# A long convolution factored 64 x 64 instead of 256 x 16, with its first and last stage as eight array pieces

## The chip, the cores and the metric

The kernel runs on one core of a Trainium2 chip. The metric is device time in microseconds (us) of one execution, the median of three runs. The names of the engines are those of the profile: PE is TensorE's matrix array and PEld its weight load, DVE is VectorE, ACT is ScalarE, POOL is GpSimd, SP is the engine that only issues transfers. DMA stands for the sixteen transfer engines that carry what SP and POOL issue.

## The reference

Two independent sequence models run on inputs of 2048 positions x 1024 channels in bfloat16. Their outputs stand side by side.

```
# A: a gated long convolution
k_shift = sum over t<4 of k_pad[:, t:t+S, :] * shift_k[:, 3 - t]
kv = k_shift * v
y  = irfft(rfft(kv, 2S) * rfft(ssm_k, 2S))[:S] + kv * ssm_D     # causal, per channel
a  = q * y
# B: a diagonal complex recurrence
Bu = einsum(x, B_bar);  h = Lam_bar * h + Bu[t] for every t
b  = 2 * Re(einsum(hs, C)) + x * Dskip
out = concatenate([a, b], -1)
```

## The kernel before, in words

**Part A** is a transform of 4096 points in two factors, done by matrix products. Before the change the factors are 256 and 16 (`N1, N2 = 256, 16`). Position s is 16 n + n2: partition n (128 of them), step n2 (16 of them).

- *kv.* `kp` and `vp` load two steps of k and v on 128 partitions each, in one transfer on SP's queue (a k block shifted by one position in two). `kvm`, `kva`, `kvb`, `kvc` form one kv tile [128, 1024] for each n2 on DVE.
- *First stage of kv.* `am` multiplies a kv tile by the 128 x 128 tables F1 (cosine, sine): four matmuls of 512 columns for each n2, 64 in all (L580). `ae` evicts each bank on ACT, `ast` stores to DRAM (Ys_kv) on POOL's queue.
- *First stage of the filter.* `hl` loads ssm_k, `hT` transposes it on PE, `hc` evicts, `hm` multiplies by F1 (128 matmuls of 256 columns, L619), `he` evicts, `hst` stores to Ys_h in two transfers (L632).
- *Second stage.* For each of 16 groups gq of two rows: `lh`, `lk` load (L642), `sh`, `sk` multiply by tables of 64 columns (two column pieces of the array side by side, L650), `she`, `ske` evict, `pr` multiplies spectra on DVE, `sa` multiplies back (two row pieces of 64 partitions, L680), `sae` evicts, `vst` stores to Vs.
- *Output stage.* `vl` loads, `a3` multiplies by the table G (two accumulating matmuls of 512 columns for each half tile, 64 in all, L706), `a3e` evicts, `qp` loads q, `qm` multiplies by q on DVE (L716), `ost` stores (L718).

All of Ys must be stored before the second stage can load, and all of Vs before the output stage: two barriers through DRAM.

**Part B** goes in 16 chunks i of 128 positions. `x` loads a transposed chunk, `U` projects it (2048 matmuls of 128 columns, L469), `ue` evicts, `r1`, `r2` rotate on DVE, `rc` adds the carry, `sc` scans, `cm`, `ca` make the next carry, `r3`, `r4` rotate back, `y` projects out (L524, L529), `ye` evicts, `yst` stores. B has no barrier, and its work lies between that of A.

**Order.** Nothing is planned while the kernel runs. The string `ORDER` is a list of some 1700 words such as `am.0.0:p6`, each a call of the function of that name, and the program is emitted in that order. Each engine and each queue then runs its own instructions strictly in that order and waits where an input or a buffer is missing. What follows the colon are the buffers: `p` is one of eight PSUM banks, `a`, `b`, `m`, `w` are rings in SBUF.

SP carries all loads, POOL all stores. At the end each engine drains (L780).

Of the kernel before, what the change touches and what calls it, by code (L numbers as in the profile page):

```python
# [67 lines left out]

ORDER = """
ld_w:a0a1 wb.3:p0 wb.2:p1 wb.0:p2 wb.1:p3 wbe.1 bl.3.1:b0 wb.7:p4 bl.3.0:b1 ld_par par_T:p5 p32 exp1 dve2 exp2 wbe.3 dve3 wbe.2 wb.4:p6 wbe.4  # L70
bl.2.1:b2 bT.2.1:p3 sm_pre bT.3.0:p5 bc.3.0 tabA1:a0a2a3a4 sin0 wbe.7 bl.4.0:b3 bT.4.0:p0 bc.4.0 bl.0.1:b4 bl.2.0:b5 bl.1.0:b6 bT.2.0:p6 wb.5:p5
bc.2.0 bT.3.1:p1 bT.0.1:p4 bl.0.0:b7 bT.0.0:p7 bc.0.0 bc.2.1 sin1 bT.1.0:p0 x.3:b8 U.3.1.0:p3 wb.6:p6 bc.3.1 U.3.1.1 bl.1.1:b9 bT.1.1:p7 bc.0.1 wbe.5
bc.1.0 wbe.6 x.1:b10 U.1.0.0:a1p5 tabA2 wbe.0 U.1.1.0:p0 U.1.1.1 x.2:b2 U.2.1.0:p2 bc.1.1 U.3.0.0:a5p7 ue.3.1 U.2.0.0:a6p3 U.2.0.1 sin2 par_rest eo
kp.1 U.2.1.1 ue.2.1 ue.2.0 z1 kp.0 dd kvm.3:m0 bl.5.0:b0 cl.2.0:b4 bT.5.0:p6 kva.3 kvb.3:b9 bc.5.0 x.0:b5 U.0.0.0:a7p4 U.0.0.1 bl.7.1:b6 U.0.1.0:p3
U.0.1.1 bl.4.1:b7 bT.4.1:p2 U.1.0.1 stt bc.4.1 ue.0.0 kp.-1 bl.5.1:b3 U.3.0.1 ue.3.0 bl.6.0:b1 ue.1.0 kvm.1:m0 cl.2.1:b11 bT.6.0:p2 bT.5.1:p4 bc.5.1
bc.6.0 U.0.2.0:p6 kva.1 kvb.1:b3 z2 cT.2.1:p5 bT.7.1:p7 bc.7.1 bl.6.1:b12 bT.6.1:p4 bc.6.1 kp.-2 kvm.0:m1 kva.0 kvb.0:b12 U.0.2.1 bl.7.0:b13 vp.0:a8
cT.2.0:p2 kvc.1 U.3.2.0:p1 cl.1.0:b14 bT.7.0:p7 U.3.2.1 bc.7.0 vp.1:a9 ue.1.1 ue.0.1 U.1.3.0:p4 U.1.3.1 U.0.3.0:p3 ue.0.2 ue.1.3 kvc.0 ld_F am.0.0:p6
cl.1.1:b0 ae.0.0:b13 U.0.3.1 ue.0.3 kvm.2:m1 cT.1.0:p4 cc.1.0 r1.0:m0 am.0.2:p6 cl.3.1:b7 cT.3.1:p0 x.4:b1 cc.3.1 ae.0.2:b7 cT.1.1:p3 cc.1.1
U.4.0.0:a8p7 cc.2.1 cl.3.0:b11 U.3.3.0:p4 U.3.3.1 ue.3.3 cT.3.0:p6 kva.2 kvb.2:b0 U.4.0.1 kvc.2 ue.4.0 cl.0.0:b6 cT.0.0:p5 cc.0.0 r2.0:a7 cl.0.1:b4
cc.2.0 sc.0.0 am.1.2:p4 am.0.1:p3 U.1.2.0:p0 ae.1.2:b6 U.1.2.1 ae.0.1 cT.0.1:p5 cc.3.0 am.1.3:p2 ast.0.0 sc.0.1 cm.0 ae.1.3 ast.1.1 r3.0:m0 r4.0  # L80
am.0.3:p7 ae.0.3 ast.0.1 U.2.2.0:p4 U.2.2.1 cc.0.1 ue.1.2 am.2.0:p2 r1.1:m1 r2.1:a0 ae.2.0:b12 U.4.3.0:p6 cx.7.0 hl.1.0:a4 U.4.3.1 ue.4.3 hl.0.0:a2
hl.0.1:a3 hT.0.0:p0 hc.0.0:b4 hl.1.1:a10 hT.1.3:p2 hT.1.0:p5 hc.1.0:b13 ld_sd hd.0 am.1.0:p6 ue.3.2 ae.1.0:b6 am.1.1:p7 ae.1.1 am.2.1:p3 ast.1.0
ae.2.1 hd.1 U.2.3.0:p0 hc.1.3:b7 hT.0.2:p5 hc.0.2:b3 U.4.2.0:p1 U.4.2.1 ue.4.2 U.2.3.1 hm.0.0.2:p2 he.0.0.2:b11 x.5:b14 U.5.0.0:a1p3 hm.0.0.3:p1
he.0.0.3 kvc.3 ca.0 rc.1 lw.2:w0 sc.1.0 hm.0.0.0:p5 he.0.0.0:b6 sc.1.1 y.0.0.0:p2 y.0.0.1 U.5.0.1 ast.2.0 hst.0.0.1 cm.1 hm.0.0.1:p5 ue.2.2 ue.2.3
r1.2:m1 hm.0.2.0:p4 cx.5.1 lw.1:w1 hm.1.0.0:p0 he.1.0.0:b4 he.0.0.1 r3.1:m0 am.2.2:p1 ae.2.2:b12 cx.4.1 am.2.3:p7 ae.2.3 y.0.0.2 y.0.0.3 hm.0.2.2:p1
hm.1.0.1:p5 cx.6.0 U.5.3.0:p7 hm.1.3.2:p0 r2.2:a6 ca.1 ast.2.1 he.1.0.1 hst.1.0.0 rc.2 hst.0.0.0 hm.1.0.3:p5 he.0.2.0:b11 hm.0.2.3:p6 hm.0.2.1:p4
he.0.2.2:b0 he.0.2.3 hst.0.2.1 U.5.3.1 r4.1 he.0.2.1 r1.3:m1 ue.5.3 sc.2.0 sc.2.1 cm.2 hT.0.3:p6 ca.2 hm.1.0.2:p4 U.5.2.0:p1 ue.5.0 he.1.3.2:b3
hT.1.2:p3 he.1.0.2:b13 r2.3:a5 rc.3 hm.1.3.0:p0 he.1.3.0:b12 he.1.0.3 hm.1.3.1:p7 he.1.3.1 y.1.0.0:p4 kp.3 hT.1.1:p0 hc.1.1:b4 hst.1.0.1 cx.6.1
hc.0.3:b6 U.5.1.0:p5 U.5.1.1 hm.1.1.3:p0 ue.5.1 cx.4.0 cx.5.0 cx.7.1 y.1.1.0:p7 hm.1.1.2:p5 ye.0.0:b0 hm.1.3.3:p6 he.1.3.3 hst.1.3.1 y.1.0.1
he.1.1.2:b7 he.1.1.3 lw.0:w2 hst.1.1.1 kp.2 kvm.4:m0 hT.0.1:p2 hc.0.1:b13 hc.1.2:b3 y.0.1.0:p6 hm.0.3.2:p0 y.0.1.1 hst.0.2.0 hm.1.1.0:p2 he.1.1.0:b5  # L90
y.0.1.2 hst.1.3.0 y.0.1.3 ye.0.1 hm.0.3.3:p5 he.0.3.2:b7 y.1.0.2 U.5.2.1 y.1.0.3 sc.3.0 ue.5.2 hl.2.1:a9 hm.0.3.0:p2 hm.0.3.1:p6 he.0.3.0:b6 kva.4
hm.1.1.1:p3 he.1.1.1 y.1.1.1 hl.2.0:a4 hT.2.3:p2 hT.2.0:p3 yst.0 he.0.3.3 he.0.3.1 hst.0.3.0 hc.2.0:b12 hm.1.2.3:p5 hm.1.2.2:p1 hst.1.1.0 he.1.2.2:b10
he.1.2.3 r3.2:m1 ye.1.0:b4 y.1.1.2 y.1.1.3 ye.1.1 U.4.1.0:p1 yst.1 U.4.1.1 hc.2.3:b0 hst.1.2.1 hm.0.1.0:p7 sc.3.1 cm.3 hst.0.3.1 ca.3 vp.4:a10 hd.2
hm.2.0.3:p4 hm.2.0.2:p2 hm.2.3.0:p5 he.2.3.0:b11 he.2.0.2:b6 he.2.0.3 hst.2.0.1 hl.3.0:a2 r4.2 y.2.0.0:p3 y.2.0.1 r3.3:m1 r4.3 hm.2.0.0:p2 he.2.0.0:b5
hm.2.3.2:p4 vp.2:a3 kvm.5:m1 hm.1.2.0:p5 hm.2.3.1:p6 he.2.3.1 hm.2.0.1:p0 he.2.0.1 kvb.4:b10 y.2.0.2 he.1.2.0:b12 ue.4.1 y.2.0.3 am.3.0:p0 ae.3.0:b4
kvm.6:m0 kva.6 hst.2.3.0 hm.0.1.1:p5 hm.1.2.1:p6 he.1.2.1 am.3.1:p1 he.0.1.0:b7 he.0.1.1 he.2.3.2:b3 hst.2.0.0 hst.0.1.0 hl.3.1:a7 hT.3.0:p2
y.2.1.0:p0 y.2.1.1 y.2.1.2 hc.3.0:b6 hst.1.2.0 am.3.2:p2 kvc.4 ae.3.1 ast.3.0 ye.2.0:b2 hd.3 hm.0.1.2:p4 hm.2.3.3:p1 hm.0.1.3:p5 he.0.1.2:b11 he.0.1.3
am.3.3:p7 y.2.1.3 am.4.3:p4 am.4.2:p5 ae.4.2:b5 ae.4.3 y.3.0.0:p3 y.3.0.1 ast.4.1 ae.3.2:b9 ae.3.3 ast.3.1 hm.3.0.2:p4 kvb.6:b0 hm.3.0.0:p2 ye.2.1
he.2.3.3 hst.2.3.1 kva.5 am.4.0:p5 ae.4.0:b12 kvb.5:b13 am.4.1:p7 kvc.5 yst.2 vp.3:a0 kvc.6 am.6.2:p6 hst.0.1.1 he.3.0.2:b10 ae.4.1 hm.3.0.3:p0
# [685 lines left out]
```

## Time and profile before

| | |
|---|---|
| median of three runs | 390.47 us (389.85 to 391.01) |
| the profiled execution | 391.46 us, of it 389.7 us of span |
| PE busy | 363.3 us, 93% of the span |
| DVE busy | 332.3 us, 85% |
| ACT busy | 278.1 us, 71% |
| POOL busy | 93.0 us, 24% |
| TensorE clock granted, mean | 0.992 |
| DMA | 92.49 MB, 237 GB/s on average |

The span is from the first to the last instruction. Durations of matmuls in the profile are modelled and overlap; how long one holds the array is seen from the distance between starts. In a row of a group the numbers behind the first bar are the group's busy time in us and the mean ns of one, behind the second bar the idle time of its engine just before them and what ended it. In a timeline row stand start, length, engine, line, operation and count.

### The profile page before, as it was taken

Reading aid. Unit: us, or ns where it says so; the run is one execution under the profiler, and the core shown is the slowest. Engines: PE = TensorE matmul, PEld = TensorE weight load, DVE = VectorE, ACT = ScalarE, POOL = GpSimd, SP = SyncE. Lnnn points to the kernel's source line nnn. Section 1 sums busy time; section 2 is a strip of 40 time slices with the busy share of each in tenths; the row PEclk is TensorE's granted clock in tenths of the full one; section 3 lists DMA queues with packets and bytes.
Section 4 is the critical chain, followed back from the end, with each engine's and each line's share of the span. In section 5 each row is a group of like instructions: output and inputs, shape, how many; then the busy total and the mean of one; then the engine's idle time right before and its main releaser. Section 6 shows DMA issues by size and latency. Waiting matters only on the chain.

```text
span 389.7 us, 9237 instructions
## 1 busy us (share of the span) xinstructions
PE 363.3 (93%) x3785; PEld 244.9 (63%) x3785; DVE 332.3 (85%) x335; ACT 278.1 (71%) x519; POOL 93.0 (24%) x156
## 2 busy tenths in 40 slices
...
GB/s 231 276 301 316 296 181 250 200 228 234 278 205 318 211 238 226 163 274 219 280 204 212 126 208 283 255 145 280 200 275 150 334 109 277 286 252 307 267 319 80
DMA packets 56005, 92.49 MB, mean 237 GB/s; under 512 B 30078, under 2 KB 32126, under 8 KB 55964
## 3 DMA queue, kind: packets, MB, share of 16 engines
...
q14 instruction: 12, 0.10, 0.1%
...
## 4 chain that ended last, share of the span: by engine, by line
PE 51%; ACT 14%; issue 12%; DVE 10%; DMA 9%; POOL 2%; POOLq 0%; ACTq 0%; DVEq 0%
PE ps_y L524 18%; PE ps_u L469 15%; PE ps_a L680 4%; PE ps_a L650 4%; DMA Ys_h<-ysbh 4%; ACT hh L657 3%; PE ps_a L619 3%; PE ps_a L580 3%; ACT xx L663 3%; DVE mt L560 2%; DMA Ys_kv<-ysb 2%; ACT vsb L687 2%; DMA out_dram<-ot 2%; DVE mt L567 2%; POOL out_dram L718 1%
## 5 line engine op out<-in xcount | busy, mean ns | idle before, releaser
L524 PE MATMUL ps_y<-CT,h 128*128 128x512 bf16 x512 | 127.0, 379 | 0.3 <-ACT ot L712 0.2
L469 PE MATMUL ps_u<-xT,BT 128*128 128x128 bf16 x2048 | 124.7, 219 | 0.6 <-ACT BT L445 0.3
L469 PEld LDWEIGHTS <-BT 128*128 128x128 bf16 x2048 | 118.4, 98 | 10.5 <-issue 4.1
L524 PEld LDWEIGHTS <-h 128*128 128x128 bf16 x512 | 45.2, 98 | 45.0 <-issue 2.4
L500 DVE TENSOR_TENSOR_SCAN h<-rtab,h 128x1024 bf16<-128x1024 f32 x32 | 71.9, 2279 | 0.3
L471 ACT CAST u<-ps_u 128x512 bf16<-128x512 f32 x64 | 38.6, 628 | 33.0 <-PE ps_u L469 24.4
L632 POOL DMA_DIRECT2D Ys_h<-ysbh x64 | 46.1, 722 | 29.0 <-ACT ysbh L625 23.3
L625 ACT CAST ysbh<-ps_a 128x512 bf16<-128x512 f32 x64 | 35.6, 616 | 16.9 <-PE ps_a L619 6.6
L481 DVE TENSOR_TENSOR mt<-u,Z 128x4096 bf16<-128x4096 bf16 x16 | 36.5, 2281 | 9.6 <-ACT u L471 9.6
L587 ACT CAST ysb<-ps_a 128x512 bf16<-128x512 f32 x64 | 35.5, 630 | 8.2 <-PE ps_a L580 4.1
L689 POOL DMA_DIRECT2D Vs<-vsb x16 | 8.5, 534 | 122.8 <-ACT vsb L687 96.7
L657 ACT CAST hh<-ps_a 128x512 bf16<-128x512 f32 x64 | 36.0, 649 | 2.3 <-PE ps_a L650 2.2
L589 POOL DMA_DIRECT2D Ys_kv<-ysb x32 | 17.5, 551 | 81.4 <-ACT ysb L587 81.4
L481 DVE TENSOR_TENSOR mt<-h,Z 128x4096 bf16<-128x4096 bf16 x16 | 36.6, 2287 | 0.2
L687 ACT CAST vsb<-ps_a 128x512 bf16<-128x512 f32 x64 | 34.2, 694 | 3.3 <-PE ps_a L680 3.3
L663 ACT CAST xx<-ps_a 128x512 bf16<-128x512 f32 x64 | 35.8, 660 | 0.6 <-PE ps_a L650 0.6
L535 ACT CAST yo<-ps_y 128x512 bf16<-128x512 f32 x32 | 19.5, 626 | 16.4 <-PE ps_y L524 16.3
L560 DVE TENSOR_TENSOR mt<-kring,wbc 128x4096 bf16<-128x4096 bf16 (+3 forms) x16 | 30.1, 1884 | 0.1
L529 PE MATMUL ps_y<-Dd,xT 128*128 128x128 bf16 x128 | 28.0, 219 | 0.0
L619 PE MATMUL ps_a<-hT,F1t 128*128 128x256 bf16 x128 | 20.5, 272 | 5.6 <-ACT hT L607 3.6
L712 ACT CAST ot<-ps_a 128x512 bf16<-128x512 f32 x32 | 17.4, 606 | 10.7 <-PE ps_a L706 6.3
L670 DVE TENSOR_TENSOR pp<-xx,hh 128x2048 bf16<-128x2048 bf16 x16 | 19.4, 1220 | 6.0 <-ACT xx L663 3.5
...
## 6 DMA issues: line engine op xcount, KB each, us to landing
...
l2h<-Ys_h SPq DMA_DIRECT2D x16, 512.0 KB, 5.7
l2k<-Ys_kv SPq DMA_DIRECT2D x16, 512.0 KB, 4.6
Vs<-vsb POOLq DMA_DIRECT2D x16, 512.0 KB, 5.4
...
kring<-in_A_k_dram SPq DMA_DIRECT2D x8, 512.0 KB, 4.3
v<-in_A_v_dram SPq DMA_DIRECT2D x8, 512.0 KB, 5.9
```

The lines of the kernel that those rows point to most:

```text
L469: nc.tensor.matmul(pu[:, w, jl, :], BT[:, 2 * jp + jl, w, d, :], xT[:, d, :], start=(d == 0), stop=(d == ND - 1))
L471: E["ue"] = lambda i, jp: nc.scalar.copy(st["u", i][:, :, 2 * jp:2 * jp + 2, :], st["pu", i, jp][:])
L481: nc.vector.tensor_mul(m, s_, win(Z))
L500: nc.vector.tensor_tensor_scan(gf, rt1, gf, 0.0, ALU.mult, ALU.add)
L524: nc.tensor.matmul(py[:], h[:, 1 - w, j, :], CT[:, j, w, dh * 512:(dh + 1) * 512], start=(j == 0 and w == 0), stop=(j == NJ - 1 and w == 1))
L560: nc.vector.tensor_mul(m[:, 0:h0, :], kring[:, s0:s0 + h0, :], wbc[:, 0:h0, :])
L587: nc.scalar.copy(st["ysb", n2, cc][:, dh * 512:(dh + 1) * 512], st["pa", n2, w][:])
L625: nc.scalar.copy(st["yh", qd, n4, w // 2][:, :, w % 2, :], st["pa", qd, n4, w][:].rearrange("p (c d) -> p c d", c=2))
L632: gpd(Ys_h[cc, n0:n0 + 2, :, qd * DQ:(qd + 1) * DQ].rearrange("n k d -> k n d"), t_[:, cc, :, :])
L657: nc.scalar.copy(st["hh", gq][:, cc, w * 512:(w + 1) * 512], st["ps", "l2h", gq, cc, w][:])
L663: nc.scalar.copy(st["xx", gq, cc][:, w * 512:(w + 1) * 512], st["ps", "l2k", gq, cc, w][:])
L687: nc.scalar.copy(st["vsb", gq][:, gi, w * 512:(w + 1) * 512], st["ps", "v", gq, w][gi][:])
```

## The change

The factors become 64 and 64. Position s is 64 n + 16 q + s': the partition is 4 n + q for the filter, and 32 q + n for k, v, q and the output, so that the four quarters q of 32 partitions hold four independent small transforms of 32 rows (n) and 64 results (32 frequencies, real and imaginary). What it does in each place:

- `am` takes two kv tiles and 512 columns: eight matmuls of 32 rows x 64 columns of the array, four row groups (one for each quarter q, each with a bank of its own) and two column groups (one for each tile). 16 calls for 64 matmuls before.
- `a3` likewise: eight matmuls of 64 rows x 32 columns, two banks, 16 calls for 64 matmuls.
- `hm` keeps 128 x 128, with a block table Fht, and takes 512 columns: 64 matmuls for 128. `hst` stores in one transfer where it took two.
- `kp`, `vp`, `qp`, `ost`: four transfers of 32 partitions each for one of 128. `lh`, `lk`, `vst`: two transfers of one group row each for one of both. `vl`: 16 transfers of 512 KB for 32 of 256 KB.
- `qm` multiplies [128, 2048], 8 times for 16.
- ost.2, ost.3 and yst.11, 13, 14, 15 are stored from SP's queue.
- The whole list `ORDER` is new. In it kv tiles 10 and 11 come last in the first stage (before: tile 14), and the store of `ost.5` is the last word.

```diff
-N1, N2, NFFT = 256, 16, 4096
-NG = 32
+N1, N2, NFFT = 64, 64, 4096
+HK = N1 // 2
+NB = 16
...
+SP_STORES = frozenset("ost.2 ost.3 yst.11 yst.13 yst.14 yst.15".split())
...
+kva.11 kvb.11:b2 kvc.11 U.11.2.0:p3 ...
+... am.5.0:p5p2p6p7 ae.5.0.0:b8 am.5.1:p4p0p3p1 ae.5.1.0 ast.5.0 U.8.1.0:p5
+U.8.1.1 ... U.11.1.0:p4 U.11.1.1 ae.5.0.3:b3 ae.5.1.3 lh.2:a7 sh.2.0.0:p3 ...
...
+... r3.15:m1 r4.15 y.15.1.0:p7 a3e.3.1.0 y.15.0.0:p5
+y.15.0.1 y.15.0.2 y.15.0.3 y.14.0.2 a3e.2.1.0 qp.6:a11 y.14.0.3 qm.6 ost.6 y.15.1.1 yst.12 y.15.1.2 qp.0:a13 qm.0 ost.0 qp.1:a3 qm.1 yst.11 ost.1
+qp.3:a7 qm.3 ost.3 a3e.2.0.1 qm.2 ost.2 y.14.1.2 y.15.1.3 ye.15.0:b6 ye.14.0:b4 ye.15.1 yst.15 y.14.1.3 ye.14.1 yst.14 ost.5
...
+    stq = lambda kind, n: spd if "%s.%d" % (kind, n) in SP_STORES else gpd
...
+    Ys_kv = tc.dram_tile([NB, HK, 2, 4, D], BF16, name="Ys_kv")
+    Ys_h = tc.dram_tile([NB, HK, 2, 4, D], BF16, name="Ys_h")
+    Vs = tc.dram_tile([NB, HK, 2, 4, D], BF16, name="Vs")
+    kr, vr, qr, oar = (a_.rearrange("(n q s) d -> q n s d", q=4, s=NB) for a_ in (k, v, q, out_a))
...
+    def quarters(t_, src, r):
+        for q_ in range(4):
+            spd(t_[32 * q_:32 * q_ + 32, :, :], src[q_, :, 2 * r:2 * r + 2, :])
...
-        st["pa", n2, w] = ptile("ps_a", [P, 512])
-        nc.tensor.matmul(st["pa", n2, w][:], F1t[:, cc, :], st["kv", n2][:, dh * 512:(dh + 1) * 512], start=True, stop=True)
+    def pieces(banks, rows, weights, cols):
+        m = weights.shape[-1]
+        for r, pt in enumerate(banks):
+            rs = slice(rows * r, rows * r + rows)
+            for j in range(P // m):
+                nc.tensor.matmul(pt[m * j:m * j + m, :], weights[rs, :], cols(j, r)[rs], start=True, stop=True)
+
+    def am(u, w):
+        st["pa", u, w] = [ptile("ps_a", [P, 512]) for _ in range(4)]
+        pieces(st["pa", u, w], 32, F1t[:], lambda j, r: st["kv", 2 * u + j][:, w * 512:(w + 1) * 512])
...
+    def ast(u, r):
+        gpd(Ys_kv[2 * u:2 * u + 2, :, :, r, :].rearrange("t k c d -> (t k c) d"), st["ysb", u, r][:])
...
+        nc.tensor.matmul(pt[:], Fht[:, kh, :], st["hT", qd, n4][:, 2 * tp:2 * tp + 2, :].rearrange("p a b -> p (a b)"), start=True, stop=True)
...
+        dst = Ys_h[4 * n4:4 * n4 + 4, 16 * kh:16 * kh + 16, :, :, qd * DQ:(qd + 1) * DQ]
+        gpd(dst.rearrange("t k c q d -> (k c q) t d"), st["yh", qd, n4, kh][:])
...
-        spd(st[nm, gq][:], Ys.rearrange("c n (s g) d -> (c n s) g d", g=NG)[:, gq * GC:(gq + 1) * GC, :])
+        for gi in range(GC):
+            spd(st[nm, gq][:, gi, :], Ys[:, gq * GC + gi, :, :, :].rearrange("t c q d -> t (c q) d"))
...
+    def vl(u, h):
+        st["vv", u, h] = k4("vv", [P, 2, D])
+        spd(st["vv", u, h][:], Vs[2 * u:2 * u + 2, :, :, 2 * h:2 * h + 2, :].rearrange("t k c q d -> (t k c) q d"))
...
+    def a3_(u, w):
+        st["po", u, w] = [ptile("ps_a", [P, 512]) for _ in range(2)]
+        pieces(st["po", u, w], 64, Gt[:], lambda j, r: st["vv", u, j // 2][:, j % 2, w * 512:(w + 1) * 512])
...
+    def ost(u):
+        for q_ in range(4):
+            stq("ost", u)(oar[q_, :, 2 * u:2 * u + 2, :], st["ot", u][32 * q_:32 * q_ + 32, :, :])
```

More of the change, by code (lines that the diff above doesn't have):

```diff
@@ L84 @@
[L84 to L87, printed above, removed]
@@ L92 @@
[L92 to L95, printed above, removed]
@@ L96 @@
[L96 to L99, printed above, removed]
@@ new lines @@
+he.1.2.0:b3 ye.1.1 hm.1.2.1:p2 he.1.2.1 y.0.1.0:p6 x.5:b0 hst.1.2.0 hm.1.1.0:p0 he.1.1.0:b9 he.1.1.1 hl.2.0:a8 r4.2 hm.1.2.3:p3 y.0.1.1 vp.4:a4
+hm.1.1.2:p2 y.0.1.2 he.1.2.2:b12 he.1.1.2:b11 hm.1.1.3:p0 hl.3.1:a10 U.5.3.0:p4 he.1.1.3 hst.1.1.1 hm.0.1.1:p0 kvb.3:b13 r3.3:m0 yst.1 U.5.1.0:p2
+y.0.1.3 he.1.2.3 ye.0.0:b14 ye.0.1 hm.0.1.0:p5 hm.0.1.2:p7 he.0.1.0:b10 he.0.1.1 hst.0.1.0 U.4.2.0:p3 hl.2.1:a5 hT.2.0:p5 hc.2.0:b3 hst.1.1.0 cm.3
+hd.2 U.4.2.1 ue.4.2 r1.4:m1 r4.3 hm.0.1.3:p0 he.0.1.2:b6 he.0.1.3 hst.0.1.1 yst.0 U.5.0.0:a0p1 lw.1:w1 vp.1:a7 kvc.3 U.5.0.1 ue.5.0 hst.1.2.1 U.5.1.1
```

347 lines of the change are left out of this document (157 added, 190 removed).

## The prediction

> **What bounds the kernel now.** The page's first part comes first, then the engines' busy time by stage, the stages cut where the first and the last matmul of the conv's second stage run (first L650, last L680) and where the last matmul ends.
>
> ```profile
> span 389.7 us, 9237 instructions
> ## 1 busy us (share of the span) xinstructions
> PE 363.3 (93%) x3785; PEld 244.9 (63%) x3785; DVE 332.3 (85%) x335; ACT 278.1 (71%) x519; POOL 93.0 (24%) x156
> ```
> ```profile
> core 0: us, PE busy (x) PEld busy (x) DVE busy (x) ACT busy (x) POOL busy (x), PEclk, DMA share, GB/s
> 0.00:183.30 183.30, 168.02 (x2099) 135.31 (x2099) 164.13 (x198) 141.88 (x250) 69.02 (x112) 1.00 0.87 244
> 183.30:317.70 134.40, 133.43 (x1234) 74.93 (x1234) 124.87 (x98) 108.51 (x217) 10.60 (x20) 1.00 0.66 218
> 317.70:380.40 62.70, 61.88 (x458) 34.68 (x456) 43.33 (x41) 27.16 (x53) 12.86 (x24) 1.00 0.82 284
> 380.40:389.70 9.30, 0.00 (x0) 0.00 (x0) 0.00 (x0) 0.57 (x1) 0.54 (x1) 0.66 0.18 67
> ```
>
> From 183.3 us to 380.4 us TensorE (PE) is busy 195.3 of 197.1 us: there its work is the time. Before 183.3 us two engines share the bound, PE with 168.0 and VectorE (DVE) with 164.1 of 183.3 us. After the last matmul 9.3 us follow in which only one eviction and one store run. So the change has to be priced three times: in PE work, in what DVE lets through in stage one, and in the end.
>
> What a matmul occupies is read from the spacing of starts, not from the modelled duration. The timeline of PE shows full-array matmuls and the two kinds of half-array pieces that the kernel has already:
>
> ```profile
> 190.00 0.22 PE L529 MATMUL ps_y<-Dd,xT 128*128 128x128 bf16 x1
> 190.06 2.97 PE L524 MATMUL ps_y<-CT,h 128*128 128x512 bf16 x13
> 192.87 0.83 PE L469 MATMUL ps_u<-xT,BT 128*128 128x128 bf16 x12
> ```
> ```profile
> 248.14 0.61 PE L680 MATMUL ps_a<-pp,wts 64*128 64x512 bf16 x4
> 248.57 0.61 PE L680 MATMUL ps_a<-hh,wts 64*128 64x512 bf16 x4
> 249.11 0.41 PE L650 MATMUL ps_a<-l2h,wts 128*64 128x512 bf16 x2
> 249.35 0.60 PE L650 MATMUL ps_a<-l2k,wts 128*64 128x512 bf16 x4
> 249.78 0.38 PE L650 MATMUL ps_a<-l2h,wts 128*64 128x512 bf16 x2
> 250.10 0.29 PE L469 MATMUL ps_u<-xT,BT 128*128 128x128 bf16 x2
> ```
>
> Thirteen full 512-column matmuls take 192.87 - 190.06 = 2.81 us, 0.216 us each; a 128-column one takes 0.06 us. Four row pieces (64*128) take 248.57 - 248.14 = 0.43 us and four column pieces (128*64) 249.78 - 249.35 = 0.43 us: two pieces run in the time of one matmul, in either direction. A change of the array's cut costs: the last row pair starts 0.22 us after 248.57 and the next kind should follow at 249.01, but starts at 249.11; the last column pair starts at 249.78 and L469 follows after 0.32 instead of 0.216 us. I take 0.10 us per change of cut.
>
> **The change part by part, on PE.**
>
> ```profile
> L619 PE MATMUL ps_a<-hT,F1t 128*128 128x256 bf16 x128 | 20.5, 272 | 5.6 <-ACT hT L607 3.6 <-ACT ysb L587 1.5
> L580 PE MATMUL ps_a<-acc,F1t 128*128 128x512 bf16 x64 | 20.1, 379 | 3.6 <-DVE mt L567 2.7 <-ACT ysbh L625 0.7 <-DVE acc L575 0.2
> L706 PE MATMUL ps_a<-vv,Gt 128*128 128x512 bf16 x64 | 16.3, 379 | 0.6 <-ACT ot L712 0.6
> ```
>
> kv's first stage (am): 64 x 0.216 = 13.8 us go; 16 calls of eight 32*64 pieces come. If all eight run side by side a call takes 0.216 us and a little for issuing eight; I take 0.24 (an estimate), 3.8 us. The new order puts the 16 calls in 13 separate places, each with a change of cut before and after: 26 x 0.10 = 2.6 us. Net -7.4 us, all in stage one.
>
> Output stage (a3): 64 x 0.216 = 13.8 us go; 16 x 0.24 = 3.8 us come, in 7 places, 14 x 0.10 = 1.4 us. Net -8.6 us, all after the second stage.
>
> The second stage's calls stay, but the new order breaks them into 30 runs of one cut where the old one has 25; with neighbours counted that is 54 changes against 44, +1.0 us. The filter's first stage (hm) has the same columns, 128 x 256 before and 64 x 512 after: 0. PE in sum: -15.0 us.
>
> The eight at once, rows and columns cut together, are in no row of this trace. From below: no call can beat one matmul, 0.216. From above: one piece after another, 8 x 0.216 = 1.73 us. The nearest rows, two kinds of pairs that both run fully side by side, lie at the lower end, so 0.24.
>
> The Trainium skill ("TensorE: Matmul & The Clock Gate", section "The cost: per-tile semaphore tail") speaks against this: where every piece counts up a semaphore when it ends, a pack ends later by some 25 + 4.7 ns a piece + 26.3 ns a count, 273 ns for eight. By it, as an estimate, the 20 places would cost 0.17 us more each and the forecast would be 3.5 us higher, still inside my own case below. The two-piece rows above show only the 0.10 us.
>
> **What stage one lets through.** The first L650 matmul stands in PE's order behind the last am call, and that needs the last kv tile, which DVE makes.
>
> ```profile
> L575 DVE TENSOR_TENSOR acc<-acc,v x16: 672/688/694, 39.2 to 176.5; 128x1024 bf16<-128x1024 bf16 x16
> ```
> ```profile
> DVE acc L573 <- PE ps_a L580: 4.1, 1, 4.1
> ```
> ```profile
> L587 ACT CAST ysb<-ps_a 128x512 bf16<-128x512 f32 x64 | 35.5, 630 | 8.2 <-PE ps_a L580 4.1 <-DMA Ys_kv<-ysb 3.9 <-PE ps_u L469 0.2
> ```
>
> The last kvc starts at 176.5 us, the second stage 6.8 us later. Counted through both orders, DVE has the same work ahead of that kvc (all 16 kv tiles, the tables, chunks 0 to 4 of the recurrence), so a lighter PE pulls it forward only by waits of DVE on PE: one of 4.1 us, for am, is in the trace. The change does not touch the rest of DVE's 19.2 idle us (183.3 - 164.1). I take -2.5 us for stage one, between 0 and PE's -7.4. That is where I part with the sum over PE: 5 us of PE's saving in stage one become waiting.
>
> What else the parts add there. Loads of k, v, q become four DMAs each (kp of a shifted block five). In stage one kp and vp go from 20 issues to 74, 54 more on SP's queue; q's loads from 8 to 32, l2 from 32 to 64, vl from 32 to 16.
>
> ```profile
> L551 SPq DMA_DIRECT2D v<-in_A_v_dram x8: 328/354/572, 25.0 to 135.1; - x8
> ```
> ```profile
> SPq L543 <- DVE mt L560: 15.9, 1, 15.9
> ```
> ```profile
> kring<-in_A_k_dram SPq DMA_DIRECT2D x8, 512.0 KB, 4.3
> ...
> kring<-in_A_k_dram SPq DMA_DIRECT2D x2, 448.0 KB, 7.4
> ...
> kring<-in_A_k_dram SPq DMA_DIRECT2D x2, 60.0 KB, 7.8
> ```
>
> An issue holds SP 0.354 us, so 54 are 19.1 us of a queue that spends much of its time waiting for a buffer (15.9 us at one kp alone), and each load's last quarter goes out 1.1 us later. I cost this at 0: behind kp and vp on SP stand loads issued ahead of need. Without that cover it is 18 loads x 1.1 = 20 us of DVE waiting. A transfer on few partitions is not slow by itself: the 60 KB on 15 partitions landed in 7.8 us beside 448 KB in 7.4 us.
>
> The Trainium skill ("SBUF — State Buffer", section on the DMA port swizzle) has 32 neighbouring partitions reach 8 of the 16 ports, so a quarter would run at half the rate. As an estimate from its 435 GB/s ceiling a quarter's 128 KB would take 0.6 instead of 0.3 us; no row here can separate that, and it is part of the transfer rival below.
>
> **Other edits, each with its cover.** hst: 32 DMAs for 64, with twice the 512-byte rows each. vst: 32 for 16. ost: 32 for 16, eight of them and four yst on SP. POOL is 24% busy and only its last issue is on the path.
>
> ```profile
> L632 POOL DMA_DIRECT2D Ys_h<-ysbh x64: 706/723/735, 67.0 to 166.3; - x64
> ```
>
> ```profile
> L513 DVE TENSOR_TENSOR h<-mt 128x2048 bf16<-128x2048 bf16 x16 | 19.5, 1220 | 0.3
> ...
> L716 DVE TENSOR_TENSOR ot<-ot,qt 128x1024 bf16<-128x1024 bf16 x16 | 10.6, 687 | 6.9 <-ACT ot L712 6.9
> ```
>
> hst costs POOL between 32 x 0.72 = 23 us and twice that (46 us, as now); 0 on the path. qm: 8 multiplications over 2048 columns (1.22 us each in r4) for 16 over 1024 (10.6 us), 0.8 us less on DVE, hidden behind PE. An am call holds four of eight banks until ScalarE has emptied them, four evictions of 35.5 / 64 = 0.55 us; PE is covered by U and y in the other four. Uncovered it is a rival, below.
>
> **The second half and the end.** From 183.3 us on PE sets the pace: -8.6 + 1.0 = -7.6 us. Then the end:
>
> ```profile
> 380.38 0.59 ACT L535 CAST yo<-ps_y 128x512 bf16<-128x512 f32 x1 [1.14 <-PE ps_y L524]
> ```
> ```profile
> 381.26 0.54 POOL L537 DMA_DIRECT2D out_dram<-yo  x1 [1.85 <-ACT yo L535]
> ```
> ```profile
> L780 POOLq EVENT_SEMAPHORE x4: 17/17/17, 388.9 to 389.6; - x4
> L780 POOLq DRAIN x3: 51/112/7653, 381.2 to 389.4; - x3
> ```
>
> Now the last store goes out on POOL, whose closing drain then lasts 7.65 us. In the new order the last stores, yst.15 and yst.14, are SP's, and POOL's last are ost.0, ost.1 and ost.5, four issues each. After the last r4, PE still has twelve quarters of y: 48 x 0.216 + 8 x 0.06 = 10.8 us. POOL meanwhile issues ost.6, yst.12, ost.0, ost.1, ost.5, 17 x 0.54 = 9.2 us, from 1.2 us after that r4 (one qm): done near 10.4. With the drain and 0.8 us of closing (388.9 to 389.7) the span ends 18.8 us after r4, 8.0 us after PE, against 9.3: -1.3 us (down to -4.3 if the drain is short when nothing is outstanding).
>
> **Sum.** 389.7 - 2.5 - 7.6 - 1.3 = 378.3 us of span. The profiled execution took 391.46 us, 1.76 more than its span, and 0.99 more than the median 390.47. 378.3 + 1.76 - 0.99 = 379.1; I give 378, since most unknowns of the end lie below.
>
> **Rivals.**
> 1. *Stage one gains in full.* The new order also takes out DVE's small waits; then PE's -7.4 comes through and the short end too: 378 - 4.9 - 3.0 = 370, down to 364 if 6 us more of the 19.2 idle go. For it: PE's largest gaps stand in stage one. Against it: DVE is 90% busy there. Chance 0.2.
> 2. *Half the gain.* New waits between PE and DVE, both near full in every stage: 384 to 389. Chance 0.1.
> 3. *Slower, the pieces do not run eight at once.* If only pairs overlap, a call is 4 x 0.216 = 0.86 us: PE changes by 32 x 0.86 - 27.6 + 4.0 + 1.0 = +5 us, 394 us; one by one it is +33, 422 us. It decides from about 0.7 us a call on. Against it: both kinds of pairs overlap fully. Chance 0.06.
> 4. *Slower, banks.* PE waits for each am's four banks: 16 x (2.2 - 0.24) = 31 us at worst, 16 at half: 394. It decides from 0.8 us of waiting a call on. Against it: ACT is 71% busy. Chance 0.06.
> 5. *Slower, transfers.* DVE waits for the last quarter of most loads: 378 + 20 = 398; it decides when 12 of the 18 come late in full. For it: in the first 183 us the DMA share is 0.87, the highest. Chance 0.06.
>
> **How the numbers follow.** My own case is 372 to 384, chance 0.49; 0.03 remain for no change. Faster (by over 0.3%, about what a measurement of this kernel can tell): 0.49 + 0.2 + 0.1 = 0.79; within 0.3%: 0.03; slower: 0.18. The range 364 to 391 leaves out 0.05 of rival 1 and most of the slower ones, 0.15.
>
> **What would show it.** PE busy near 348 us; the eight pieces of a call starting within 0.1 us, the next call of the same cut 0.22 to 0.26 us after; 94 changes of cut at 0.10 us. The first matmul of L650's counterpart near 181 us with the last kvc near 174; the second half near 189 us; POOL's drain after ost.5. I am wrong if a call takes over 0.5 us, if DVE's waits name kring, v or am's evictions with more than 8 us, or if the second stage starts after 184 us.

## The result

The changed kernel takes 366.87 us (median of 4 runs, 366.3 to 367.39) against 390.74 us (4 runs, 389.85 to 393.51) for the kernel before: a ratio of 0.9377, 95% interval 0.9328 to 0.9427. The forecast was 378, range 364 to 391. The time lies in the stated range but below the prediction's own case of 372 to 384; what came is the case of rival 1: stage one gains in full, and some more. A ratio compares only runs within 1.5% of the fastest run of the same kernel on the same chip, so that it can differ from the quotient of two medians, most of all in e4 to e7, where just two of the seven runs of the kernel before count (387.2 and 390.58 us; the others took 393.64 to 395.95).

The first part of the changed kernel's page, then the engines' busy time by stage, cut at the same places as before (first L648 matmul, last L678, end of the last matmul):

```profile
span 364.5 us, 9501 instructions
PE 346.6 (95%) x3849; PEld 227.9 (63%) x3849; DVE 329.0 (90%) x327; ACT 281.4 (77%) x521; POOL 81.8 (22%) x145
```
```profile
core 0: us, PE busy (x) PEld busy (x) DVE busy (x) ACT busy (x) POOL busy (x), PEclk, DMA share, GB/s
0.00:169.30 169.30, 160.92 (x2097) 125.26 (x2097) 160.00 (x196) 145.00 (x253) 47.13 (x80) 1.00 0.94 265
169.30:295.10 125.80, 124.64 (x1159) 67.91 (x1158) 117.28 (x94) 107.59 (x214) 18.80 (x36) 1.00 0.83 232
295.10:356.90 61.80, 61.08 (x596) 34.72 (x595) 51.68 (x39) 28.27 (x55) 15.88 (x30) 1.00 0.87 272
356.90:364.50 7.60, 0.00 (x0) 0.00 (x0) 0.00 (x0) 0.58 (x1) 0.00 (x0) 0.80 0.65 207
```

The span is 25.2 us shorter. PE's work is 363.3 - 346.6 = 16.7 us less, and the span outside PE's work 26.4 - 17.9 = 8.5 us less. By stage:

| stretch | before | after | difference | of it PE work | of it PE idle |
|---|---|---|---|---|---|
| stage one | 183.3 | 169.3 | -14.0 | -7.1 | -6.9 |
| second half, to the last matmul | 197.1 | 187.6 | -9.5 | -9.6 | +0.1 |
| after the last matmul | 9.3 | 7.6 | -1.7 | | -1.7 |

VectorE's (DVE's) idle time in stage one fell with it, from 19.2 to 169.3 - 160.0 = 9.3 us; its busy time fell by 4.1 us though its instructions are the same but for two tiny ones (the sum of their durations is 175.4 and 174.5 us): records of instructions in direct succession overlap a little, and time that two records share is counted once. B's work on PE in stage one is the same too, 1376 matmuls of U and 160 of L506 (L524 before). DVE's last wait of over 0.3 us in stage one, on its timeline, ends before 28 us, and the last kvc, the counterpart of the row at 176.5 us, is now at 163.8. From 40 us on both engines are full, in 40 to 120 us PE with 80.0 and DVE with 79.5 of 80 us (75.0 and 73.4 before):

```profile
27.59 4.50 DVE L549 TENSOR_TENSOR mt<-kring,wbc 128x4096 bf16<-128x4096 bf16 x2 [2.44 <-ACT wbc L406]
```
```profile
L564 DVE TENSOR_TENSOR acc<-acc,v x16: 671/683/692, 35.8 to 163.8; 128x1024 bf16<-128x1024 bf16 x16
```
```profile
40.00:80.00 40.00, 40.00 (x504) 31.35 (x501) 39.65 (x33) 34.34 (x56) 10.73 (x16) 1.00 0.97 256
80.00:120.00 40.00, 40.00 (x407) 26.27 (x406) 39.83 (x37) 33.79 (x61) 14.97 (x24) 1.00 0.87 277
```

The eight pieces on PE's timeline, one am call between full matmuls, two a3 calls in a row, and then two am calls in a row with what follows them:

```profile
129.28 1.24 PE L506 MATMUL ps_y<-CT,h 128*128 128x512 bf16 x5
130.45 0.42 PE L572 MATMUL ps_a<-acc,F1t 32*64 32x512 bf16 x8
130.80 0.39 PE L617 MATMUL ps_a<-hT,Fht 128*128 128x512 bf16 x1
```
```profile
340.56 0.63 PE L572 MATMUL ps_a<-vv,Gt 64*32 64x512 bf16 x16 [0.57 <-ACT yo L517]
341.12 0.82 PE L506 MATMUL ps_y<-CT,h 128*128 128x512 bf16 x3
```
```profile
152.69 1.15 PE L572 MATMUL ps_a<-acc,F1t 32*64 32x512 bf16 x16
153.98 0.33 PE L451 MATMUL ps_u<-xT,BT 128*128 128x128 bf16 x3
```
```profile
L572 PE MATMUL ps_a<-acc,F1t 32*64 32x512 bf16 x128 | 7.6, 395 | 0.2
L572 PE MATMUL ps_a<-vv,Gt 64*32 64x512 bf16 x128 | 5.0, 381 | 0.7 <-ACT yo L517 0.6
```

Five full matmuls from 129.28 on are due to end their turn at 130.36 (5 x 0.216); the pack starts at 130.45, 0.09 us later. The next matmul starts 0.35 us after the pack's first piece, where a full matmul would have held PE 0.216. So one lone call costs 0.216 + 0.09 + 0.13, and two calls in a row take 0.56 us with their way out. The eight run at once: the 128 pieces of am are busy 7.6 us, where the rows of the 64 full matmuls showed 20.1 (13.8 by the spacing of starts); a3's 5.0 instead of 16.3. The idle time before them is 0.2 and 0.7 us, but that is not all their waiting. The last six am calls come as three pairs, and a pair holds PE 1.29 (153.98 - 152.69), 1.23 and 1.34 us where a pair of a3 takes 0.56: its pieces start in several bursts. That is 2.2 us over the price of three pairs, inside the busy time. By the list each of these pairs needs all eight banks (`am.5.0:p5p2p6p7`, `am.5.1:p4p0p3p1`), so banks not yet emptied are the likely cause; no run isolates it.

How it ends. First SyncE's (SP's) queue on the timeline, then GpSimd's (POOL's) and SP's closing rows:

```profile
350.57 8.24 SPq L716 DMA_DIRECT2D out_dram<-ot  x8
358.91 1.53 SPq L519 DMA_DIRECT2D out_dram<-yo  x2
```
```profile
L779 POOLq DRAIN  x3: 46/108/5882, 355.8 to 364.3; - x3
L779 SPq DRAIN  x3: 7/7/13, 363.7 to 364.0; - x3
```

POOL's long drain runs from 355.8 for 5.9 us, to 361.7. SP is later: its eight issues of ost.3 and ost.2 take 8.24 us together, so that yst.15 leaves at 358.91 and yst.14 after it, and SP passes its closing waits only at 363.7. The last stores' queue, not POOL's drain, now holds the end.

### The profile page after: what moved, and what is told of

It is laid out like the page before. It is cut to its first block, busy times and chain, and to the rows that moved or that the text cites. A ratio compares the mean times of both kernels' runs of the same rounds, so it can differ in the third digit from the quotient of the medians.

```text
span 364.5 us, 9501 instructions
## 1 busy us (share of the span) xinstructions
PE 346.6 (95%) x3849; PEld 227.9 (63%) x3849; DVE 329.0 (90%) x327; ACT 281.4 (77%) x521; POOL 81.8 (22%) x145
## 4 chain that ended last, share of the span: by engine, by line
PE 80%; ACT 9%; DMA 5%; issue 2%; POOL 1%; DVE 1%; ACTq 0%; POOLq 0%; DVEq 0%
PE ps_u L451 27%; PE ps_y L506 27%; PE ps_a L678 8%; PE ps_a L648 8%; PE ps_a L617 4%; PE ps_t L600 2%; DMA out_dram<-ot 2%; PE ps_a L572 2%; ACT BT L427 2%; DMA xT<-in_B_x_dram 2%; PE ps_y L511 2%; ACT ysb L582 1%; PE ps_t L416 1%; ACT wbc L406 1%; POOL out_dram L716 1%
## 5 line engine op out<-in xcount | busy, mean ns | idle before, releaser
L451 PE MATMUL ps_u<-xT,BT 128*128 128x128 bf16 x2048 | 123.4, 219 | 4.1 <-ACT wbc L406 2.1
L451 PEld LDWEIGHTS <-BT 128*128 128x128 bf16 x2048 | 117.2, 98 | 14.3 <-issue 8.5
L506 PE MATMUL ps_y<-CT,h 128*128 128x512 bf16 x512 | 125.8, 380 | 0.0
L506 PEld LDWEIGHTS <-h 128*128 128x128 bf16 x512 | 44.7, 98 | 50.7 <-issue 8.2
L453 ACT CAST u<-ps_u 128x512 bf16<-128x512 f32 x64 | 37.6, 623 | 19.9 <-PE ps_u L451 19.3
L624 ACT CAST ysbh<-ps_a 128x512 bf16<-128x512 f32 x64 | 34.6, 608 | 8.9 <-PE ps_a L617 7.8
L689 POOL DMA_DIRECT2D Vs<-vsb x32 | 16.9, 535 | 95.2 <-ACT vsb L685 92.3
L582 ACT CAST ysb<-ps_a 128x512 bf16<-128x512 f32 x64 | 34.0, 619 | 2.2 <-PE ps_a L572 2.2
L629 POOL DMA_DIRECT2D Ys_h<-ysbh x32 | 24.1, 753 | 50.5 <-ACT ysbh L624 50.3
L648 PEld LDWEIGHTS <-wts 128*64 128x64 bf16 x256 | 13.7, 109 | 14.6 <-issue 5.8
```

Source lines behind the costliest of these rows:

```text
L451: nc.tensor.matmul(pu[:, w, jl, :], BT[:, 2 * jp + jl, w, d, :], xT[:, d, :], start=(d == 0), stop=(d == ND - 1))
L453: E["ue"] = lambda i, jp: nc.scalar.copy(st["u", i][:, :, 2 * jp:2 * jp + 2, :], st["pu", i, jp][:])
L506: nc.tensor.matmul(py[:], h[:, 1 - w, j, :], CT[:, j, w, dh * 512:(dh + 1) * 512], start=(j == 0 and w == 0), stop=(j == NJ - 1 and w == 1))
L582: nc.scalar.copy(st["ysb", u, r][:, w * 512:(w + 1) * 512], st["pa", u, w][r][:])
L624: nc.scalar.copy(st["yh", qd, n4, kh][:, 2 * tp:2 * tp + 2, :].rearrange("p a b -> p (a b)"), st["ph", qd, n4, w][:])
L648: nc.tensor.matmul(pt[64 * gi:64 * gi + 64, :], st["w", gq][:, gi, 64 * cc:64 * cc + 64], st[nm, gq][:, gi, w * 512:(w + 1) * 512], start= ...
```

## The experiments

They ran on three chips, on which the kernel before took 394.0 us (e1, e2, e9, e10), 393.8 (e4 to e7) and 392.8 us (e3, e8, e10b, e11) in the median of all its runs. Spans are set beside the changed kernel's 364.5 or the old one's 389.7, whose chip is not on record; in stages that an edit did not reach they agree within 0.3 us in e2, e5 and e6 and within 1.4 us in the others, the limit of such a comparison. e10 and e10b are worse: the old stage one, which their edit leaves alone, takes 187.6 and 186.1 us there instead of 183.3.

**e1: PE's old work back in stage one.** In the changed kernel, ahead of every am call:

```diff
     def am(u, w):
         st["pa", u, w] = [ptile("ps_a", [P, 512]) for _ in range(4)]
+        for pt in st["pa", u, w]:
+            nc.tensor.matmul(pt[:], ident[:], st["kv", 2 * u][:, w * 512:(w + 1) * 512], start=True, stop=True)
         pieces(st["pa", u, w], 32, F1t[:], ...)
```


> The changed kernel, with four additional full 128x512 matmuls (by the identity, overwritten by the pieces) before each am call, so that the first stage of kv costs PE what it did before: +16 x 4 x 0.216 = +13.8 us of PE, and some 0.6 us of more changes of cut. Theory P (PE paces stage one; the old order had waits of its own there): all of it passes, 366.9 + 14 = 381 us, and the second stage starts at about 183 instead of 169.3 us. Theory D (the prediction's: DVE gates stage one, a third of PE's work there passes): 366.9 + 5 = 372 us, second stage from 174 us.

```profile
0.00:183.15 183.15, 173.33 (x2143) 129.78 (x2162) 164.05 (x199) 145.96 (x253) 47.11 (x80) 1.00 0.91 245
```

378.72 us (377.75 to 379.82), ratio 0.9642 [0.9592, 0.9692]. Stage one is 183.15 - 169.3 = 13.85 us longer for 13.8 us of matmuls: in the new order, work on PE in stage one passes to the end whole, or nearly so (12.95 us for the same edit in e3).

**e2: the same in the output stage.** Four full matmuls ahead of each a3 call, two into each of its two banks, 13.8 us again.

```diff
+        for pt in st["po", u, w] * 2:
+            nc.tensor.matmul(pt[:], ident[:], st["vv", u, 0][:, 0, w * 512:(w + 1) * 512], start=True, stop=True)
         pieces(st["po", u, w], 64, Gt[:], ...)
```


> The changed kernel, with four additional full 128x512 matmuls before each a3 call: +13.8 us of PE after the second stage and some 1.8 us of more changes of cut. Both theories have PE as the pace there: 366.9 + 15.6 = 382 us. If the tail is instead held by DVE's last chunks or by the stores, less: 372 to 377 us.

```profile
295.10:371.80 76.70, 75.72 (x650) 40.49 (x660) 52.12 (x39) 29.01 (x55) 15.96 (x30) 1.00 0.72 232
371.80:375.70 3.90, 0.00 (x0) 0.00 (x0) 0.00 (x0) 0.58 (x1) 0.00 (x0) 0.80 0.40 149
```

378.98 us (377.52 to 379.87), ratio 0.9644 [0.9593, 0.9695]. The last part is 14.9 us longer, but the end after PE shrinks from 7.6 to 3.9 us: with more time, the stores catch up. So of PE's gain at the very end some 3.7 us are lost again to the stores.

**e3: both.** The edits of e1 and e2 together.

> The changed kernel with four full-array matmuls ahead of each am call and of each a3 call (their results are overwritten), so that all 27.6 us of PE work that the old form had come back: 128 x 0.216. Theory P (the gain of this change is PE work, the new order only lets it through): the time is that of the kernel before, within 4 us, a ratio of 0.99 to 1.01. Rival O (the new order brings a good part of the gain by itself, by taking out waits, of which 6.9 us of idle PE in stage one were seen to go): 4 to 12 us below the kernel before, a ratio of 0.97 to 0.99. By the sum of the two single experiments, 366.9 + (378.7 - 366.9) + (379.0 - 366.9) = 390.8 us.

```profile
0.00:182.25 182.25, 177.21 (x2161) 132.56 (x2161) 164.06 (x199) 145.99 (x253) 47.26 (x80) 1.00 0.90 246
182.25:307.30 125.05, 124.25 (x1158) 67.82 (x1156) 113.50 (x91) 107.44 (x214) 18.49 (x35) 1.00 0.83 234
307.30:384.30 77.00, 76.96 (x664) 40.52 (x660) 52.40 (x40) 29.32 (x55) 16.31 (x31) 1.00 0.73 233
384.30:388.20 3.90, 0.00 (x0) 0.00 (x0) 0.00 (x0) 0.59 (x1) 0.00 (x0) 0.96 0.36 135
```

390.39 us (389.04 to 391.77), ratio 0.9976 [0.9936, 1.0017]: theory P's number. But my expectation had overlooked that this kernel holds more than the old PE work: the pieces and their changes of cut are still there. PE is busy 177.2 + 124.3 + 77.0 = 378.4 us, 15.1 more than in the kernel before, in a span 1.5 us shorter; PE's idle time is 388.2 - 378.4 = 9.8 instead of 26.4 us. So the run does not clear the order of its share. Between e3 and the changed kernel 31.8 us of PE work moved the span by 23.7, 0.75 a us; by that rate the new order with exactly the old work would stand near 388.2 - 15.1 x 0.75 = 377 us, so that order and pieces would have about half of the gain each. That is an estimate: no kernel here has it.

**e9: the lighter PE in the old order.** The kernel before with am's matmuls and the columns that its evictions read cut to a quarter, which leaves out three quarters of kv's first stage.

```diff
-        nc.tensor.matmul(st["pa", n2, w][:], F1t[:, cc, :], st["kv", n2][:, dh * 512:(dh + 1) * 512], start=True, stop=True)
+        nc.tensor.matmul(st["pa", n2, w][:, 0:128], F1t[:, cc, :], st["kv", n2][:, dh * 512:dh * 512 + 128], start=True, stop=True)
```


> The kernel before, in its own order, with each of the 64 am matmuls cut from 512 to 128 columns (the evictions copy those 128 columns four times, so three quarters of kv's first stage are left out): PE loses 64 x 0.16 = 10.2 us in stage one, and nothing else changes. Theory D: a third passes, 390.7 - 3.4 = 387 us. Theory P: nearly all passes, 380 to 382 us. If the old order can't use it at all: 390 us.

```profile
0.00:176.40 176.40, 160.00 (x2091) 133.29 (x2099) 164.27 (x198) 141.48 (x250) 68.67 (x111) 1.00 0.88 253
```

385.07 us (381.85 to 388.28), ratio 0.9776 [0.9702, 0.9849]. Stage one is 6.9 us shorter for 10.2 us less of PE by the spacing of starts (8.0 in the busy column): two thirds or more pass even in the old order, where the prediction let a third through. The ratio alone, which does not lean on one trace, says 6 to 12 us. DVE does the same work, and its idle time falls from 19.2 to 12.1 us. Its waits up to 176 us, in the kernel before and in e9:

```profile
DVE acc L573 <- PE ps_a L580: 4.1, 1, 4.1
DVE hT L612 <- DMA sd<-in_A_ssm_D_dram: 2.2, 1, 2.2
DVE hT L612 <- ACT hT L607: 1.6, 1, 1.6
```
```profile
DVE acc L573 <- PE ps_a L580: 1.0, 1, 1.0
...
DVE hT L612 <- ACT hT L607: 0.5, 1, 0.5
```

The wait that names PE gives 3.1 us. Another 3.3 us come from two waits that name a DMA and ACT: the one for sd is gone altogether. Its issue stands on POOL behind kv's stores, these behind ACT's evictions, and these behind PE's am. That chain is read from the order; no run isolates it. What the traces show is the total at this place: 3.8 us before, 6.2 in e10 and 2.7 in e10b, where stage one is untouched (and no wait there names sd), and 0.5 in e9.

**e10 and e10b: the same in the output stage of the old order**, a3's matmuls at a quarter of the columns, which leaves out three quarters of the output sums; run twice.

```diff
-            nc.tensor.matmul(pt[:], Gt[:, cc, :], st["vv", n2][:, cc, w * 512:(w + 1) * 512], start=(cc == 0), stop=(cc == 1))
+            nc.tensor.matmul(pt[:, 0:128], Gt[:, cc, :], st["vv", n2][:, cc, w * 512:w * 512 + 128], start=(cc == 0), stop=(cc == 1))
```


> The kernel before, in its own order, with each of the 64 a3 matmuls cut from 512 to 128 columns (three quarters of the output stage's sums are left out): PE loses 10.2 us in the last 50 us. Both theories, PE paces the second half: 390.7 - 10 = 381 us. If stores, POOL's queue or the loads of Vs hold the tail instead: 386 to 390 us.

> The same kernel as e10, for a clean trace: the kernel before with the matmuls of the output stage 128 instead of 512 columns wide, which leaves out three quarters of the sums of the output stage, 10.2 us less of PE work after the second stage. If the second half is PE's in the old order as well, the last matmul ends 9 to 10 us earlier than the 380.4 us of the kernel before; if ScalarE's evictions or the stores set the pace there, 4 to 7 us earlier, with the waits of PE naming them.

The last part in the trace of e10b:

```profile
320.00:382.40 62.40, 56.29 (x460) 33.25 (x456) 43.74 (x41) 27.28 (x53) 12.89 (x24) 0.95 0.80 279
```
```profile
PE ps_a L706 <- ACT ot L712: 3.9, 2, 3.6
```

387.12 us (ratio 0.9834 [0.9754, 0.9913]) and 393.83 us (387.15 to 394.21, no ratio). In both profiled executions the granted clock was lower (0.974 and 0.975 on the mean, 0.992 in the kernel before), so their spans cannot be set beside 389.7. What can be read is that PE stood idle 6.1 us in this part (0.8 in the kernel before) and waited 3.9 us for ScalarE's (ACT's) evictions of ot. That a lighter a3 is not worth its full 10.2 us in the old order is likely by this, and not settled. Taken together, e9 and e10 took 20.4 us of PE work from the old order and gained 2.2% and 1.7%, some 15 us: 0.75 a us, the rate that e3 gave from the other side, though with an interval of up to 6 us either way.

**e5: more DVE work in stage one.** The changed kernel with kvb made twice for every other tile, 8 x 0.69 = 5.5 us.

```diff
         nc.vector.tensor_add(st["kv", n2][:], m[:, 0, :], m[:, 1, :])
+        if n2 % 2 == 0:
+            nc.vector.tensor_add(st["kv", n2][:], m[:, 0, :], m[:, 1, :])
```


> The changed kernel with kvb done twice for eight of the sixteen kv tiles: 8 x 0.69 = 5.5 us more DVE work in stage one, the same values. Theory D (DVE gates stage one): all of it passes, second stage from about 175 us, 372 us in all. Theory P (PE paces it, DVE follows with slack): 0 to 2 us, 367 to 369 us.

```profile
0.00:176.20 176.20, 165.89 (x2099) 129.60 (x2099) 166.52 (x204) 145.60 (x253) 47.16 (x80) 0.99 0.92 255
```

372.75 us (371.84 to 374.1), ratio 0.9588 [0.9501, 0.9675]; stage one 6.9 us longer for 6.5 us more of DVE (166.5 - 160.0), the later stages as they were. Together with e1: in stage one neither engine hides the other. Either one's added work comes out at the end, though PE is idle 8.4 and DVE 9.3 us of it: most of that idle time lies in the first 28 us.

**e8: more DVE work in the second stage.** Also in the changed kernel:

```diff
-        nc.vector.tensor_mul(st["pp", gq, cc][:], ...)
+        for _ in range(2 if cc == 0 and gq % 2 == 0 else 1):
+            nc.vector.tensor_mul(st["pp", gq, cc][:], ...)
```


> The changed kernel with one of the four products of the second stage made twice in every other group: 8 more DVE instructions of 1.22 us, 9.8 us, between 169 and 295 us, PE's work as it is. Theory (in the second stage PE alone sets the pace, and DVE's 8.5 idle us take up the rest): 0 to 4 us longer. Rival (there too both are at the bound, as in stage one): 8 to 10 us longer.

```profile
170.30:302.60 132.30, 126.16 (x1157) 68.16 (x1156) 125.54 (x101) 107.94 (x214) 18.48 (x35) 1.00 0.79 220
```
```profile
188.59 0.37 PE L679 MATMUL ps_a<-pp,wts 64*128 64x512 bf16 x1 [0.68 <-DVE pp L669]
...
276.14 0.61 PE L679 MATMUL ps_a<-pp,wts 64*128 64x512 bf16 x4 [0.54 <-DVE pp L669]
277.47 0.61 PE L679 MATMUL ps_a<-hh,wts 64*128 64x512 bf16 x4 [0.72 <-DVE hh L669]
```

374.91 us (373.93 to 376.44), ratio 0.9607 [0.9536, 0.9678], 8.0 us above the changed kernel; the second stage is 6.5 us longer and PE now waits for pp and hh. The rival came: in this stage too DVE's 8.5 idle us take up only part of 9.8 us of added work.

**e4: the quartered loads alone.** The kernel before, with k, v and q loaded 32 partitions at a time and nothing else.

```diff
-            spd(t_, kr[:, 2 * r:2 * r + 2, :])
+            quarters(t_, kr, r)
...
+    def quarters(t_, src, r):
+        for q_ in range(4):
+            spd(t_[32 * q_:32 * q_ + 32, :, :], src[32 * q_:32 * q_ + 32, 2 * r:2 * r + 2, :])
```


> The kernel before with every load of k, v and q issued as transfers of 32 partitions (54 more issues on SP in stage one, 24 more later), nothing else changed. The prediction's cost of 0: within 1 us of the kernel before. Rival 5 (DVE waits for the last quarter of most loads): 10 to 20 us slower.

The first 40 us of the kernel before, and those of e4; then the waits of DVE and of PE in e4:

```profile
0.00:40.00 40.00, 33.92 (x518) 31.08 (x518) 32.56 (x83) 33.48 (x57) 2.60 (x10) 1.00 1.05 278
```
```profile
0.00:40.00 40.00, 29.27 (x400) 26.08 (x401) 27.81 (x78) 27.96 (x50) 2.61 (x10) 0.96 0.78 202
```
```profile
DVE mt L565 <- DMA kring<-in_A_k_dram: 13.8, 2, 9.0
...
PE ps_t L434 <- DMA ld<-in_B_B_re_dram: 11.5, 2, 5.8
```

397.56 us (397.25 to 400.35), ratio 1.0239 [1.013, 1.0348]: slower, and by how much is not sharp. Every run is above all seven of the kernel before on that chip (387.2 to 395.95), whose median of 393.8 is 0.9% lower; in the trace the second stage starts 6.1 us later, at 189.4. The loss lies in the first 80 us, where loads are what everybody waits for; the DMA engines move 202 instead of 278 GB/s in the first 40. Whether SP's longer queue of issues or the transfers of 32 partitions themselves are to blame was not separated. In the changed kernel no wait of DVE is for a load of kring or v.

**e11: one wait taken out of the old order.** The load of sd moved some 40 us up in the kernel before's order, the only edit.

```diff
-... hc.1.0:b13 ld_sd hd.0 am.1.0:p6 ...
+... hc.1.0:b13 hd.0 am.1.0:p6 ...
-... kvc.0 ld_F am.0.0:p6 ...
+... kvc.0 ld_F ld_sd am.0.0:p6 ...
```


> The kernel before with the one load of sd moved from behind hT's turn to just behind F1's load, some 40 us earlier in the order: DVE waited 2.2 us for it at 60 us, and PE stood 3.3 us at 61 us behind the same chain. If the idle time in the old stage one is a chain of such single waits, each on the path, the second stage starts 2 to 3.3 us earlier (180 to 181.3) and the time falls by as much, 0.5 to 0.8%. If the next wait takes its place, nothing changes: within 1 us.

PE's waits on the timeline of the kernel before, then of e11:

```profile
64.33 0.38 PE L619 MATMUL ps_a<-hT,F1t 128*128 128x256 bf16 x2 [3.32 <-ACT hT L607]
...
122.31 0.38 PE L619 MATMUL ps_a<-hT,F1t 128*128 128x256 bf16 x2 [1.47 <-ACT ysb L587]
```
```profile
60.77 0.38 PE L619 MATMUL ps_a<-hT,F1t 128*128 128x256 bf16 x2 [0.24 <-ACT hT L607]
...
121.03 0.59 PE L619 MATMUL ps_a<-hT,F1t 128*128 128x256 bf16 x2 [3.02 <-ACT ysb L587]
```

391.32 us (387.85 to 398.94), ratio 0.9995 [0.9946, 1.0044]: no difference. The wait went (3.32 us became 0.24, and the matmul behind it came 3.6 us earlier), and by 121 us most of the lead was given back to the next one, which grew from 1.47 to 3.02 us. The second stage starts at 182.25, 1.0 us earlier. (In e10b, with the old order and the load of sd in its old place, this same wait is 2.54 us, at 121.82; part of the growth may be the spread between executions.) The idle time of the old stage one is not a list of waits that can be struck out one by one.

**e6 and e7: the end.** e6 sends all stores by POOL's queue; e7 sends yst.14 and yst.15 by ACT's and leaves the other four on SP's.

```diff
-SP_STORES = frozenset("ost.2 ost.3 yst.11 yst.13 yst.14 yst.15".split())
+SP_STORES = frozenset()
```


> The changed kernel with all stores on POOL, as before (SP_STORES empty). The last store, yst.14, is then POOL's, and its drain of 6 to 8 us begins after it: the end after the last matmul grows from 7.6 to 9 or 10 us, 368 to 370 us. If the six stores on SP gain nothing: 367 us.


```diff
-    stq = lambda kind, n: spd if ...
+    stq = lambda kind, n: nc.scalar.dma_start if (kind, n) in (("yst", 14), ("yst", 15)) else spd if ...
```


> The changed kernel with the last two stores, yst.14 and yst.15, issued from ACT's queue, where nothing stands ahead of them; in the changed kernel yst.14 waits on SP behind eight issues of ost.3 and ost.2 that take up to 1.7 us each, 2.2 us after its eviction has ended. If that queue is what holds the end: 2 to 2.5 us less, 364.5 us. If POOL's drain holds it as well (it ended at 361.7 us of 364.5): 1 to 2 us less. If the landing of all stores holds it: no change.

POOL's drain in e6, then two rows of e7: its stores of ot, and the wait of SP for a store of yo.

```profile
L779 POOLq DRAIN  x3: 46/108/4905, 362.1 to 367.5; - x3
```
```profile
L716 SPq DMA_DIRECT2D out_dram<-ot x8: 316/427/697, 351.4 to 363.3; - x8
```
```profile
SPq L716 <- DMA out_dram<-yo: 8.6, 2, 8.4
```

e6: 370.0 us (369.34 to 371.24), ratio 0.9523 [0.9409, 0.9637]; the last matmul ends at 356.6 as in the changed kernel, the span 11.2 us after it instead of 7.6: POOL's last store and its drain come later. SP's stores are worth 3 to 4 us. e7: 369.57 us (368.57 to 370.1), ratio 0.95 [0.942, 0.958]: no gain. ACT issues both stores at once, but SP's last four issues of ot now wait 8.4 us for an earlier store and leave from 361.9 us on; its last matmul also ends 1.3 us later, at 358.2, for a reason not looked into. No version faster than the changed kernel was found.

## Why the prediction was right, and where not

- **PE's work** (-15.0 forecast): -16.7. Output stage: -8.6 forecast; 64 x 0.216 = 13.8 us became 5.0 in L572 and seven ways in at 0.09, -8.2. Stage one: -7.4 forecast, -7.1 came, in part by luck. am's own rows, 13.8 - 7.6 - 13 x 0.09, give only 5.0, since the three pairs wait. Some 1.9 of the rest lies in the rows of U and y, the same matmuls as before but busy 84.1 -> 83.0 and 41.2 -> 40.4 us, which the forecast had no term for and whose cause is open. The second stage, priced at +1.0 for more changes of cut, does not show: the second half lost 9.6, which leaves -1.4 beside a3, assigned to no term.
- **Eight at once, 0.24 a call and 0.10 a change:** right, but for the three pairs. Two changes around a lone call measure 0.09 + 0.13. The Trainium skill ("TensorE: Matmul & The Clock Gate", section "The cost: per-tile semaphore tail") would have a pack in which all eight pieces count up a semaphore end, as an estimate, 273 ns later. No pack of this trace is that case, so it is not tested: in the ten lone am calls one to five of the eight pieces count, and in every one the next matmul starts 0.33 us after the last piece, 0.12 more than between full matmuls, whatever the number.
- **"What stage one lets through" (-2.5):** the step that failed, by 11.5 us of the 13.8 that the span came out below the forecast. It let PE's saving through only by the wait of DVE that names PE, 4.1 us. e9 shows the mistake: with the same DVE work that wait shrinks by 3.1, as thought, and waits under the names of a DMA and of ACT by 3.3 more; that PE stood at the head of their chains too is the reading of the order, argued and not isolated. e1 and e5 show the state afterwards, both engines on the path. The other 6.9 us, PE's idle time, went with the new order, whose DVE has its last longer wait of stage one before 28 us; e11 shows that they were not to be had by taking out one wait, and how much of the whole gain is the order's stays an estimate (e3).
- **The second half is PE's:** right for the sum, but not for the reason. e8 shows that DVE's work counts there too.
- **Loads at 0:** right in the changed kernel, where DVE waits for no load of kring or v, and not because the loads have cover: in the old order the same quarters held the second stage up by 6.1 us (e4). Rival 5's mechanism exists; what keeps it from deciding in the new order was not tested.
- **Pieces one by one (rival 3) and banks at 0 (rival 4):** the first did not happen, eight pieces start at once. The second likely happened in small: some 2 us inside three pairs of am, against the 16 us of that rival's half case.
- **The end (-1.3):** -1.7, by another mechanism. The forecast had POOL's drain after ost.5 last, 8.0 us after PE. It ends 4.8 us after PE; SP's eight slow issues of ot (up to 1.7 us each) hold yst.14, and so the end, at 7.6.
